# Decay attention and a softplus feed-forward on one core: attention chunks in pairs of two batches

## The chip, the cores and the metric

The kernel runs on one core of a Trainium2 chip. The metric is the device time of one execution in microseconds; three runs of the kernel before gave a median of 625.59 us (625.25 to 626.13). TensorE is called PE below, VectorE DVE, ScalarE ACT, GpSimd POOL, and SP is the engine whose queue issues nearly all DMAs.

## The reference

```python
# q, k, v: (batch 4, heads 8, seq 768, head_dim 64), float32
gamma = 1.0 - 2.0 ** (-5.0 - np.arange(H))          # one decay per head
for t in range(S):
    state = gamma * state + outer(k[t], v[t])        # 64 x 64 per batch and head
    y[t] = q[t] @ state / sqrt(D)
x = y as (3072 tokens, 512)                          # heads side by side
h = x @ w_in                                         # 512 -> 2048
g = np.maximum(h, 0.0) + np.log1p(np.exp(-np.abs(h)))   # softplus
out = g @ w_out                                      # 2048 -> 512
```

The two weight matrices arrive as 64-bit floats, everything else as 32-bit floats.

## The kernel before, in words

**Feed-forward.** The 3072 tokens are worked off in six blocks of 512. A block has 16 steps, one for each 128 of the 2048 hidden features. A step's *hidden group* is 12 matmuls of 128x512 (four slices of x, three products of high and low parts each) into one of two PSUM banks, hp0 and hp1. Then L660 (DVE) and L661 (ACT) make the softplus' correction in the buffer sp, of which there is one; L662 (DVE) reads hp a last time and finishes softplus in sp; L663 (ACT) rounds it to gh and L664 (POOL) takes the remainder to gl. The step's *acc groups* are eight matmuls of gh and four of gl with w_out, into the four banks acc0 to acc3, one for each 128 tokens. After 16 steps acc goes out through w0 or w1. The matmuls of both kinds stand under L343, the helper `mm`.

**Weights.** In block 0 each weight slice is loaded as 64-bit words and turned into a high and a low part (L367 to L391); this uses a bank of a0, a1 for a short while.

**Attention.** The sequences are cut into chunks of 128 positions, six for each batch, 24 in all, four for one block of tokens. `unit` makes one chunk: q, k and v of all heads are loaded (L418, L421) into the buffers qn, kn, vn (two of each), q and v are scaled by powers of the decay (L430, L434), and then PE visits the chunk:

- *transposes* of q and k (T128, L479: four 128x128 for each; or in merged units 64-row pieces, L459), which ACT copies into kt (L486, L487);
- *scores* (Q64): 64x64 matmuls, four side by side, for the scores and for the k-v products of both half chunks. DVE masks the scores into ah (L505) and adds the products to the running state (L514, L516), one state buffer for each half chunk;
- *y* (Q64): state times q, and scores times v. From the sixth unit on ACT copies one part out (L591), DVE adds the other (L597), ACT rounds to x (L600), POOL takes the remainder (L601). Before that L566 and L567 do it.

A visit needs two PSUM banks, of a0, a1 (in the start-up of other banks too). From the twelfth unit on (`MERGED`) the y of a chunk and the transposes of the next one are one planned operation, and the two banks of each step are taken from a0, a1, hp0, hp1 (`WIDE`). `flush` emits a y that is still pending.

**Order.** Nothing is emitted directly. Every operation is given to `Planner` with an engine, a cost, what it comes after, the buffers it uses and a due time, and the planner simulates the five engines: it always takes the operation that can start first, and among those that can start at that time the one with the earliest due time, then the lower number. The resulting order is the order of each engine's queue, SP's DMAs included. An operation that uses several banks starts when all are given back, and a bank is given back when every operation on it has been planned. `waits` holds an operation back for a rival with an earlier due time that wants the same banks within `RESERVE`, or `HOLD` for a patient one. Due times come from a running `now` that advances by 5.44 us a step; `LEAD`, `STAGE` and `EXTRA` place the three steps of a unit against it, `UNIT` and `STEP0` do so in the start-up, whose sequence is `ORDER`. `SLOW` multiplies the costs of ACT, DVE and POOL in the simulation. Each matmul then waits on the chip only for what it itself reads or writes.

In the due times a step's hidden group and the acc groups of the step before it stand side by side:

```python
o = PE(m_ * matmul_time(width, P), group, xs + list(ws) + lasts[-1:], [hp], when[0] + len(lasts))
...
o = PE(m * matmul_time(DM, P), group, need, [acc, gh, gl], when[1] + seq)
...
ffn_step(None, None, i, f, (now - early * step, now + hidden_time + second_time))
```

Of the kernel before, what the change touches and what calls it, by code (L numbers as in the profile page):

```python
# [30 lines left out]
MERGED = 11  # L31
HOLD = 1000
# [21 lines left out]
ENTER = {"R128": 0, "T128": 0, "Q64": 121, "F128": 0}  # L54
LEAVE = {"R128": 0, "T128": 24, "Q64": 202, "F128": 0}
# [46 lines left out]
class Planner:  # L102
# [13 lines left out]
    def order(self):  # L116
# [30 lines left out]
        while len(out) < len(self.ops):  # L147
            best, fits, wants = None, {}, []
            for e, cands in ready.items():
                fits[e] = []  # L150
                for since, op in cands:
                    b = begin(op, since)
                    if op.patient:
                        wants += [(op.due, max(free[e], since), op, u) for u in op.uses if u.slot is None and u.among[0] in SHARED]
                    if b < 1e12:
                        s = max(free[e], b)
                        fits[e].append((s, b, op))
                        if not op.patient:
                            wants += [(op.due, s, op, u) for u in op.uses if u.slot is None and u.among[0] in SHARED]

            def waits(s, op):
                for u in op.uses:
                    if u.slot is None and u.among[0] in SHARED:
                        rivals = sum(d < op.due and t < s + (HOLD if o.patient else RESERVE) and o is not op and not set(v.among).isdisjoint(u.among) for d, t, o, v in wants)
# [58 lines left out]
UNIT = 3000  # L223
STEP0 = 4500
LEAD = -4000
STAGE = 3400
EXTRA = 0.5
# [4 lines left out]
SLOW = 1.02  # L232
# [4 lines left out]
COMFORT = {'PE': 0, 'ACT': 100, 'DVE': 100, 'POOL': 100, 'SP': 0}  # L237
# [3 lines left out]
def decay_attention_then_softplus_ffn(ctx: ExitStack, tc: tile.TileContext, q, k, v, w_in, w_out, qtab, vtab, gtab, out):  # L241
# [53 lines left out]
    hold_st = holder(pool, [P, ND, D], F32, *slots("st", ST))  # L295
# [100 lines left out]
    xdone, xread, stlast, states, ys, pending = {}, {}, {}, {}, [], []  # L396

    def unit(m, first, G, when):

        n = len(ys) + len(pending)  # L400
# [40 lines left out]
        merged = n >= MERGED  # L441
        wide = lambda merged: WIDE if merged and len(ATT[0]) == 2 else ATT[0]
# [6 lines left out]
        i, off = divmod(m * C, T)  # L449
        xt = X[i % 2]  # L450
# [3 lines left out]
        if merged:  # L454
# [6 lines left out]
            tdeps, tuses = ldk + [dq] + old(KT), [*tp, kn, qn]  # L461
            if pending:
                outputs_, cost_, deps_, uses_, _, finish_ = pending.pop()[1:]

                def outputs_and_turn():
                    outputs_()
                    turn()

                tk = tq = PE(cost_ + 58 * 2 * E, outputs_and_turn, deps_ + tdeps, uses_ + tuses, when[0], "Q64")
                tk.patient = True  # L470
                finish_(tk)
            else:
                tk = tq = PE(58 * 2 * E, turn, tdeps, tuses, when[0], "Q64")
            turned = lambda i: bank(tp[i])[:, :2 * E * D].rearrange("p (s e t) -> p s e t", s=2, e=E)
            into = lambda i: buf(kt)[:, :, :E, part(i)]
        else:
# [4 lines left out]
            tk = PE(109 * E, lambda: transposes(0, kn), ldk + old(KT), [tp[0], kn], when[0], "T128")  # L481
            tq = PE(109 * E, lambda: transposes(1, qn), [dq] + old(KT), [tp[1], qn], when[0], "T128")
# [20 lines left out]
        s = PE(2 * E * 117, scores, ck + old(AH) + [dv, *ldk], [kt, kn, vn] + sc, when[1], "Q64")  # L503
# [5 lines left out]
        rows = lambda held: buf(held).rearrange("p (a g) d -> p a g d", a=2)[:, :, first:first + G]  # L509
# [13 lines left out]
        def record(done):  # L523
            for j in range(es.start, es.stop):
                xdone[m, j] = list(done[j % 2])

        if n < FENCED:
            def outputs():
# [8 lines left out]
                def state(r, i, g, a):  # L537
                    add(r, i, g, a, (buf(st[i])[side[r], 2 * a + first + g], buf(kt)[side[r], 1, a * G + g, part(i)]))
# [22 lines left out]
            def finish(y):  # L561
                ys.append(y)
                xdeps = [o for j in range(es.start, es.stop) for o in xread.get((i - 2, j), [])]
# [5 lines left out]
        else:  # L569
            xs = hold_xs()  # L570

            def outputs():
                for g in range(G):
                    for i in range(2):
                        for a in range(2):
                            for r in range(2):
                                if st[i] is not None:
                                    mm(first_half(yp[r])[side[a], 2 * g + i], buf(st[i])[side[r], 2 * a + first + g], buf(kt)[side[r], 1, a * G + g, part(i)], True, True)
# [8 lines left out]
            def finish(y):  # L587
                ys.append(y)
                xdeps = [o for j in range(es.start, es.stop) for o in xread.get((i - 2, j), [])]
# [14 lines left out]
        deps = ma + su[:1] + [dv] + ck + (stlast[m - 1] if c else [])  # L604
        uses = yp + [vn, ah, kt] + [x for x in st[:2] if x]
        pending.append((m, outputs, cost, deps, uses, when[2], finish))
        if n + 1 < MERGED:
            flush()

    def flush():  # L610
        if pending:
            m, outputs, cost, deps, uses, due, finish = pending.pop()
            finish(PE(cost, outputs, deps, uses, due, "Q64"))
# [4 lines left out]
    def ffn_step(s, h, i, f, when):  # L618
        if pending and pending[0][0] < NT * (i + 1):
            flush()  # L620
# [72 lines left out]
        for t in ts:  # L693
# [8 lines left out]
            r = slice(i * T + t * P, i * T + (t + 1) * P)  # L702
# [130 lines left out]
```

## Time and profile before

| | |
|---|---|
| median of three runs | 625.59 us |
| profiled execution: its own time / span of its instructions | 626.27 us / 624.5 us |
| granted PE clock | 1.000 |
| busy PE / DVE / ACT / POOL | 614.5 / 242.3 / 226.7 / 239.8 us |
| HBM traffic | 35.66 MB read, 6.29 MB written |
| wide matmuls (hidden; acc with gh; acc with gl): mean start to start in a row of 12 | 2.72 us for 12 |

In the lines of the profile an instruction is named by its line in the kernel, its engine, its operation and `output<-inputs`, where the names are those of buffers and banks without their numbers. A row of the timeline is start, time until the last one's end, and a count; rows of PE overlap, since matmuls are pipelined and their ends are modelled, so start-to-start is what counts. The square bracket holds the idle time of the engine before the row and what ended it. In the list of waits a line is who waited for whom, the total, the times and the longest. A queue's own lines (SPq) are DMA issues.

### The profile page before, as it was taken

To read this page: it belongs to the slowest core of one execution; us is meant where nothing else is said; L and a number is where in the kernel's file an instruction comes from. 1 tells how busy PE (TensorE), PEld (TensorE's weight loads), DVE (VectorE), ACT (ScalarE), POOL (GpSimd) and SP (SyncE) were. 2 spreads that over 40 slices of the span, in tenths; PEclk is the share of its full clock that TensorE was granted. 3 is DMA by queue.
4 is the path that set the end of the run, shared out by engine and by line. 5 is a ranking of instruction groups with operands and counts; after the bars stand their busy time and mean duration, and the time that the engine had idled before them with its cause. 6 is when DMAs were issued, how large, how long until landed. Compare 5 with 4: busy or idle time off the path is not lost.

```text
span 624.5 us, 13208 instructions
## 1 busy us (share of the span) xinstructions
PE 614.5 (98%) x5619; PEld 500.4 (80%) x5619; DVE 242.3 (39%) x438; ACT 226.7 (36%) x407; POOL 239.8 (38%) x206
## 2 busy tenths in 40 slices
PE   8799999999999999999999999999999999999997
PEld 5678788878888888888888888888888888888886
DVE  3677878643233233332333323324323232322232
ACT  3757778532323233233232332332323331322221
POOL 3667778642233243242332323423323222222221
PEclk9999999999999999999999999999999999999999
DMA  7998385232012023020221210202400000100001
GB/s 187 250 278 257 103 264 186 52 99 72 14 38 52 1 53 102 18 51 8 45 52 68 52 35 18 51 7 45 120 1 18 2 2 0 68 1 1 0 1 67
DMA packets 90442, 42.80 MB, mean 69 GB/s; under 512 B 77072, under 2 KB 85264, under 8 KB 90384
## 3 DMA queue, kind: packets, MB, share of 16 engines
q1 hardware_dynamic: 89936, 41.95, 24.5%
q8 instruction: 44, 0.72, 0.5%
q14 instruction: 14, 0.11, 0.1%
q10 hardware_dynamic: 448, 0.01, 0.0%
HBM read 35.66 MB, written 6.29 MB: 67 GB/s over the span
## 4 chain that ended last, share of the span: by engine, by line
PE 94%; DMA 2%; SPq 2%; ACT 1%; issue 0%; POOL 0%; DVE 0%; POOLq 0%; DVEq 0%
PE hp L343 44%; PE acc L343 42%; PE a L343 5%; PE hp L459 1%; SPq L421 1%; DMA raw<-in_moe_w_out_dram 1%; PE a L479 1%; DMA vn<-in_v_dram 1%; DMA qn<-in_q_dram 0%; SPq L360 0%; SPq L418 0%; PE hp L743 0%; POOL win L391 0%; PE acc L479 0%; DVE sp L660 0%
## 5 line engine op out<-in xcount | busy, mean ns | idle before, releaser
L343 PE MATMUL hp<-x,win 128*128 128x512 f32 (+1 forms) x1176 | 296.2, 388 | 0.1
L343 PEld LDWEIGHTS hp<-x,win 128*128 128x128 f32 x1176 | 215.6, 188 | 44.4 <-DVE x L567 0.3
L664 POOL TENSOR_TENSOR gl<-sp,gh 128x512 fp32r<-128x512 f32 x90 | 116.3, 1293 | 282.7 <-ACT gh L663 205.3
L343 PE MATMUL acc<-wout,gh 128*128 128x512 f32 x736 | 198.9, 393 | 0.6 <-DVE x L567 0.5
L343 PEld LDWEIGHTS acc<-wout,gh 128*128 128x128 f32 x736 | 136.3, 188 | 29.9 <-DVE x L567 0.6
L661 ACT ACTIVATE sp<-sp 128x512 f32<-128x512 f32 x92 | 58.1, 631 | 247.6 <-DVE sp L660 247.6
L660 DVE TENSOR_SCALAR sp<-hp 128x512 uint32<-128x512 uint32 x92 | 63.6, 691 | 188.5 <-PE hp L343 119.2
L343 PE MATMUL acc<-wout,gl 128*128 128x512 f32 x368 | 102.7, 391 | 0.0
L662 DVE SCALAR_TENSOR_TENSOR sp<-hp,sp 128x512 f32<-128x512 f32 x92 | 63.5, 691 | 52.6 <-ACT sp L661 52.2
L343 PEld LDWEIGHTS acc<-wout,gl 128*128 128x128 f32 x368 | 68.8, 188 | 14.9 <-POOL gl L664 0.4
L663 ACT CAST gh<-sp 128x512 fp32r<-128x512 f32 x90 | 55.8, 620 | 56.6 <-DVE sp L662 56.5
L601 POOL TENSOR_TENSOR x<-xs,x 128x512 fp32r<-128x512 f32 x20 | 25.6, 1280 | 37.6 <-ACT x L600 37.5
L597 DVE TENSOR_TENSOR xs<-a,xs 128x256 f32<-128x256 f32 (+1 forms) x40 | 14.3, 400 | 55.7 <-ACT xs L591 55.7
L434 POOL TENSOR_TENSOR qn<-qn,tabs 128x512 f32<-128x512 f32 (+1 forms) x23 | 23.7, 1031 | 17.0 <-DMA qn<-in_q_dram 17.0
L430 POOL TENSOR_TENSOR vn<-vn,tabs 128x512 f32<-128x512 f32 (+1 forms) x24 | 24.2, 1007 | 6.4 <-DMA vn<-in_v_dram 6.3
L367 ACT ACTIVATE raw<-raw 128x512 f32<-128x512 f32 x32 | 21.7, 678 | 10.9 <-DMA raw<-in_moe_w_out_dram 5.5
L391 POOL TENSOR_TENSOR wout<-w,wout 128x512 fp32r<-128x512 f32 x16 | 20.7, 1293 | 6.4 <-ACT wout L390 6.2
L391 POOL TENSOR_TENSOR win<-w,win 128x512 fp32r<-128x512 f32 x16 | 20.7, 1295 | 3.2 <-ACT win L390 3.1
L382 DVE SCALAR_TENSOR_TENSOR a<-raw,a 128x512 uint32<-128x512 uint32 x28 | 19.0, 691 | 1.2 <-ACT a L371 0.7
L387 DVE SCALAR_TENSOR_TENSOR w<-raw,a 128x512 uint32<-128x512 uint32 x28 | 18.7, 682 | 1.0
L600 ACT CAST x<-xs 128x512 fp32r<-128x512 f32 x20 | 12.4, 619 | 14.5 <-DVE xs L597 14.5
L343 PEld LDWEIGHTS a<-kt,st 64*64 64x64 f32 x616 | 11.2, 134 | 7.7 <-issue 6.7
(117 smaller groups left out, 404.6 us busy)
## 6 DMA issues: line engine op xcount, KB each, us to landing
raw<-in_moe_w_in_dram SPq DMA_DIRECT2D x16, 512.0 KB, 5.9
raw<-in_moe_w_out_dram SPq DMA_DIRECT2D x16, 512.0 KB, 6.1
qn<-in_q_dram SPq DMA_DIRECT2D x44, 128.0 KB, 3.2
kn<-in_k_dram SPq DMA_DIRECT2D x44, 128.0 KB, 2.8
vn<-in_v_dram SPq DMA_DIRECT2D x22, 256.0 KB, 3.3
out_dram<-w SPq DMA_DIRECT2D x22, 256.0 KB, 2.1
out_dram<-win SPq DMA_DIRECT2D x2, 256.0 KB, 2.1
qn<-in_q_dram SPq DMA_DIRECT2D x4, 64.0 KB, 2.4
```

Source lines behind the costliest of these rows:

```text
L343: mm = lambda o, l, r, start, stop: emit(nc.tensor.matmul(o, lhsT=l, rhs=r, start=start, stop=stop))
L367: a = ACT(685, lambda word=word: emit(nc.scalar.activation(word(1).bitcast(F32), word(1).bitcast(F32), AF.Copy, scale=2.0**-112)), [ld], [ ...
L382: lambda word=word, wp=wp: emit(nc.vector.scalar_tensor_tensor(bits(wp), word(1), 0x80000000, bits(wp), op0=ALU.bitwise_and, op1=ALU.bitwi ...
L391: low_ = POOL(1300, lambda nm=nm, w=w: emit(nc.gpsimd.tensor_tensor(hl(nm, f)[:, 1], buf(w), hl(nm, f)[:, 0].bitcast(F32), op=ALU.subtract ...
L430: emit(engine.tensor_tensor(heads(held), heads(held), by, op=ALU.mult))
L434: emit(engine.tensor_tensor(all_, all_, by, op=ALU.mult))
L601: xl = POOL(2.53 * E * C, lambda: emit(nc.gpsimd.tensor_tensor(xo(1), buf(xs)[:, :E], xo(0).bitcast(F32), op=ALU.subtract)), [xh] + xdeps, ...
L660: a = DVE(vector_time(T), lambda: emit(nc.vector.tensor_scalar(U(spv()), U(bank(hp)), 0x80000000, None, op0=ALU.bitwise_or)), [lasts[-1]] ...
L661: b = ACT(640, lambda: emit(nc.scalar.activation(spv(), spv(), AF.Softplus)), [a], [sp])
L662: c = DVE(vector_time(T), lambda: emit(nc.vector.scalar_tensor_tensor(spv(), bank(hp), 0.0, spv(), op0=ALU.max, op1=ALU.add)), [b], [hp, sp])
L663: e = ACT(scalar_time(T, False), lambda: emit(nc.scalar.copy(buf(gh), spv())), [c], [sp, gh])
L664: g = POOL(1300, lambda: emit(nc.gpsimd.tensor_tensor(buf(gl), spv(), buf(gh).bitcast(F32), op=ALU.subtract)), [e], [sp, gh, gl])
```

## The change

- Positions 0 to 23 are run through in another order: `TURN` maps position p to chunk m so that batches 0 and 1 take turns chunk by chunk, then batches 2 and 3. Block i of the feed-forward takes positions 4i to 4i+3, and the output rows follow.
- From position 8 on (`PAIRED`) two positions, the same chunk of two batches, are made together. `unit` has become a generator that yields each PE operation's cost, work, predecessors and buffers; `units` joins those of its members into one operation. A pair has three visits: transposes of both (a new kind, S128), scores of both, y of both. The even position has the banks hp0 and hp1 for all three, the odd one a0 and a1; the even one's matmuls are emitted first. Merging y with the next transposes, `pending` and `flush` are gone; positions 4 to 7 are units by themselves as before.
- The state after the first half of a chunk is written into the chunk's k buffer, which is therefore held until y; state buffers are now one for each chunk.
- In `waits`, a patient operation counts as a rival only once the return of its banks is planned, and the time for which it holds others back is 200 ns plus a tenth of its lateness.
- Constants: `UNIT` 3000 to 3400, `STEP0` 4500 to 5600, `LEAD` -4000 to 0, `STAGE` 3400 to 6000, `EXTRA` 0.5 to 0.25, `SLOW` 1.02 to 1.0, `COMFORT` of ACT, DVE and POOL 100 to 0.

```diff
-MERGED = 11
-HOLD = 1000
+PAIRED = 8
+HOLD = 200
...
-                        rivals = sum(d < op.due and t < s + (HOLD if o.patient else RESERVE) and ...
+                        rivals = sum(d < op.due and t < s + (HOLD + max(0.0, s - d) / 10 if o.patient else RESERVE) and ...
...
+    TURN = [NC * (2 * g + a) + c for g in range(B // 2) for c in range(NC) for a in range(2)]
...
-        if (m, 0) not in states:
-            states[m, 0], states[m, 1] = hold_st(), hold_st() if c < NC - 1 else None
-        st = states[m - 1, 1] if c else None, states[m, 0], states[m, 1]
+        if m not in states:
+            states[m] = hold_st() if c < NC - 1 else None
+        st = states[m - 1] if c else None, kn, states[m]
...
-        tp = [hold_bank(wide(merged)) for _ in range(2)]
-        sc = [hold_bank(wide(merged)) for _ in range(2)]
-        yp = [hold_bank(wide(n + 1 >= MERGED)) for _ in range(2)]
+        wide = [["hp0", "hp1"], ["a0", "a1"]][p % 2] if paired and len(ATT[0]) == 2 else ATT[0]
+        tp, sc, yp = [[hold_bank(wide) for _ in range(2)] for _ in range(3)]
...
+            tk = tq = yield 58 * 2 * E, turn, ldk + [dq] + old(KT), [*tp, kn, qn], when[0], "S128"
...
+        s = yield 2 * E * 117, scores, ck + old(AH) + [dv, *ldk], [kt, kn, vn] + sc, when[1], "Q64"
...
+        y = yield cost, outputs, ma + su[:1] + [dv] + ck + (stlast[m - 1] if c else []), yp + [vn, ah, kt] + [x for x in st[:2] if x], when[2], "Q64"
+        finish(y)
+
+    def units(*members):
+
+        running = [unit(*args, len(members) > 1) for args in members]
+        asked = [next(r) for r in running]
+        while asked:
+            costs, runs, deps, uses, dues, kinds = zip(*asked)
+            op = PE(sum(costs), runs[0] if len(runs) == 1 else lambda runs=runs: [run() for run in runs], [d for ds in deps for d in ds], [x for xs in uses for x in xs], min(dues), kinds[0])
+            op.patient = len(members) > 1
+            asked = []
+            for r in running:
+                try:
+                    asked.append(r.send(op))
+                except StopIteration:
+                    pass
...
-            while m < min(target + EXTRA, NB * NT):
-                unit(m, 0, 2, [now + LEAD, now + LEAD + STAGE, now + LEAD + 2 * STAGE])
-                m += 1
+            while m < min(target + EXTRA, NT * (i + 2)):
+                whens = [now + LEAD, now + LEAD + STAGE, now + LEAD + 2 * STAGE]
+                if m >= PAIRED:
+                    units((m, 0, 2, whens), (m + 1, 0, 2, whens))
+                    m += 2
+                else:
+                    units((m, 0, 2, whens))
+                    m += 1
```

More of the change, by code (lines that the diff above doesn't have):

```diff
@@ L157, in order @@
                         fits[e].append((s, b, op))
-                        if not op.patient:
-                            wants += [(op.due, s, op, u) for u in op.uses if u.slot is None and u.among[0] in SHARED]
+                        wants += [(op.due, s, op, u) for u in op.uses if u.slot is None and u.among[0] in SHARED]
             def waits(s, op):
@@ L163, in waits @@
                     if u.slot is None and u.among[0] in SHARED:
-                        rivals = sum(d < op.due and t < s + (HOLD if o.patient else RESERVE) and o is not op and not set(v.among).isdisjoint(u.among) for d, t, o, v in wants)
+                        rivals = sum(d < op.due and t < s + (HOLD + max(0.0, s - d) / 10 if o.patient else RESERVE) and o is not op and not set(v.among).isdisjoint(u.among) for d, t, o, v in wants)
                         if rivals and rivals >= sum(opens(n, op.engine) <= s for n in u.among):
@@ L236 @@
 RAMP = 8
-COMFORT = {'PE': 0, 'ACT': 100, 'DVE': 100, 'POOL': 100, 'SP': 0}
+COMFORT = {'PE': 0, 'ACT': 0, 'DVE': 0, 'POOL': 0, 'SP': 0}
 @with_exitstack
@@ L393, in convert_weights, with unit @@
             wdone[nm, f] = hi, low_
-    xdone, xread, stlast, states, ys, pending = {}, {}, {}, {}, [], []
-    def unit(m, first, G, when):
-        n = len(ys) + len(pending)
+    xdone, xread, stlast, states, ys, count = {}, {}, {}, {}, [], [0]
+    TURN = [NC * (2 * g + a) + c for g in range(B // 2) for c in range(NC) for a in range(2)]
+    def unit(p, first, G, when, paired):
+        n = count[0]
+        count[0] += 1
+        m = TURN[p]
         b, c = divmod(m, NC)
@@ L448, in unit @@
         side = (lo, up)
-        i, off = divmod(m * C, T)
-        xt = X[i % 2]
+        block, off = divmod(p * C, T)
+        xt = X[block % 2]
         old = lambda by: [ys[n - by]] if n >= by else []
         part = lambda i: slice(i * D, (i + 1) * D)
-        if merged:
+        if paired:
             def turn():
@@ L524, in record @@
             for j in range(es.start, es.stop):
-                xdone[m, j] = list(done[j % 2])
+                xdone[p, j] = list(done[j % 2])
         if n < FENCED:
@@ L537, in state @@
                 def state(r, i, g, a):
[L538 removed]
+                    add(r, i, g, a, (state_of(st[i])[side[r], 2 * a + first + g], buf(kt)[side[r], 1, a * G + g, part(i)]))
                 def inner(r, i, g, a):
@@ L562, in finish @@
                 ys.append(y)
-                xdeps = [o for j in range(es.start, es.stop) for o in xread.get((i - 2, j), [])]
+                xdeps = [o for j in range(es.start, es.stop) for o in xread.get((block - 2, j), [])]
                 xo = lambda t, r: xt[:, t, off // W, es.start + r:es.stop:2, off % W:off % W + C]
@@ L588, in finish @@
                 ys.append(y)
-                xdeps = [o for j in range(es.start, es.stop) for o in xread.get((i - 2, j), [])]
+                xdeps = [o for j in range(es.start, es.stop) for o in xread.get((block - 2, j), [])]
                 xo = lambda t: xt[:, t, off // W, es, off % W:off % W + C]
@@ L766, in decay_attention_then_softplus_ffn @@
             first, G = (0, 2) if len(item) == 2 else (int(item[2]), 1)
-            unit(int(item[1]), first, G, [now, now + 1500, now + 2200])
+            units((int(item[1]), first, G, [now, now + 1500, now + 2200]))
             now += UNIT * G
```

56 lines of the change are left out of this document (15 added, 41 removed).

## The prediction

> **What bounds the kernel now.** I read the page first (busy times, the slices, the chain of work that ended last), then the list of waits, then TensorE's timeline around one attention unit, and last what the other engines do at the same moment.
>
> ```profile
> span 624.5 us, 13208 instructions
> PE 614.5 (98%) x5619; PEld 500.4 (80%) x5619; DVE 242.3 (39%) x438; ACT 226.7 (36%) x407; POOL 239.8 (38%) x206
> PE   8799999999999999999999999999999999999997
> PEclk9999999999999999999999999999999999999999
> PE 94%; DMA 2%; SPq 2%; ACT 1%; issue 0%; POOL 0%; DVE 0%; POOLq 0%; DVEq 0%
> ```
>
> TensorE (PE) is full from the third slice on and is 94% of the chain; no other engine passes 39%. So the time is the sum of what PE issues plus the few moments in which it waits, and the change must be priced as PE time: what a visit to attention costs, how many there are, and whether PE now waits inside one. The next fence, from the chain in order of time and then PE's timeline, shows one whole period.
>
> ```profile
> 177.18 2.72 PE hp L343 x12
> 202.21 2.72 PE hp L343 x12
> 162.84 2.88 PE L343 MATMUL hp<-x,win 128*128 128x512 f32 x12
> 165.56 1.98 PE L343 MATMUL acc<-wout,gh 128*128 128x512 f32 x8
> 167.38 1.07 PE L343 MATMUL acc<-wout,gl 128*128 128x512 f32 x4
> 168.38 0.69 PE L343 MATMUL a<-kt,st 64*64 64x64 f32 x32
> 168.89 0.65 PE L343 MATMUL a<-ah,vn 64*64 64x64 f32 x32
> 169.47 0.46 PE L459 MATMUL hp<-ident,kn 64*128 64x64 f32 x8
> 169.77 0.42 PE L459 MATMUL hp<-ident,qn 64*128 64x64 f32 x8
> 170.11 1.20 PE L343 MATMUL acc<-wout,gh 128*128 128x512 f32 x4
> 171.15 1.53 PE L343 MATMUL hp<-x,win 128*128 128x512 f32 x6
> 172.51 0.61 PE L343 MATMUL acc<-wout,gh 128*128 128x512 f32 x2
> 173.57 0.22 PE L343 MATMUL hp<-vn,kn 64*64 64x64 f32 x2
> 173.98 0.23 PE L343 MATMUL hp<-vn,kn 64*64 64x64 f32 x2
> 174.15 0.96 PE L343 MATMUL hp<-x,win 128*128 128x512 f32 x3
> 174.95 0.62 PE L343 MATMUL acc<-wout,gh 128*128 128x512 f32 x2
> 176.10 1.08 PE L343 MATMUL acc<-wout,gl 128*128 128x512 f32 x4
> ACT kt L486 <- PE hp L459: 11.2, 14, 1.0
> ```
>
> What to see. Twelve wide matmuls take 2.72 us, 0.227 each. From 177.18 to 202.21 are 25.03 us; four steps of 24 wide matmuls are 21.76 of them, so 3.27 us is what one unit costs. *Scores visit*: the two acc matmuls at 172.51 end at 172.96, the next wide one starts at 174.15, which is 1.19, and its group of three takes 0.80 instead of 0.68: 1.31 in all. The scores go in groups of four side by side; seven groups lie between 173.57 and 173.98, 0.0586 each, so 16 groups are 0.94 and 0.37 is the price of going in and out. *Merged visit* (y of one chunk, transposes of the next): 167.38 plus four matmuls is 168.29, the next wide one is at 170.11: 1.82, and four that take 1.04 instead of 0.91: 1.95. It holds 0.94 of y, 0.37 of in and out, and 0.64 for the transposes: eight pairs side by side, four pairs in 0.30 with the slow first one (so about 0.065 a pair, 0.5 together) and 0.14 for one more change of array layout. 1.95 + 1.31 is 3.26, the whole 3.27: PE doesn't wait at all here. The last line says that there are 14 merged visits.
>
> **The change, part by part.** *Visits.* Positions 8 to 23 become eight pairs of three visits, 24. For the same chunks there are now 14 merged visits, 16 for scores, two for y alone (the first chunk's and the last's) and two for transposes alone, 34. The older form of transposes is this:
>
> ```profile
> 144.32 0.60 PE L479 MATMUL a<-ident,kn 128*128 128x128 f32 x4
> 144.75 0.60 PE L479 MATMUL a<-ident,qn 128*128 128x128 f32 x4
> 145.11 1.17 PE L343 MATMUL hp<-x,win 128*128 128x512 f32 x4
> ```
>
> That is 0.79, and 0.10 more in the wide matmuls after it (four take 1.17 here, 1.07 at 167.38): 0.89. Before, in sum: 14 x 1.95 + 16 x 1.31 + 2 x 1.31 + 2 x 0.89 = 52.7 us. After, for a pair: scores 32 groups x 0.0586 + 0.37 = 2.25; y the same, 2.25; transposes 16 pairs x 0.065 + 0.37 = 1.41. The last is an operation that never stands alone in this trace. Its going in and out lies between nothing beyond the work (it can't be under 1.0) and the 0.64 - 0.5 = 0.14 of a layout change added to 0.37, so 1.0 to 1.55; I take Q64's 0.37, because the same wide matmuls stand on both sides. A pair is 5.91, eight are 47.3. Gain on paper: 52.7 - 47.3 = 5.4 us, with ends 4.3 and 8.7.
>
> The Trainium skill, TensorEngine Tiling (Array Packing), Key Properties, says that changing the tiling mode drains the array. The rows agree (0.37 for two changes). By that rule alone one counts changes, ten for two units before and six for a pair; at half of 0.37 each the four saved would be 0.74 a pair, an estimate of 5.9 us for eight pairs beside 5.4 from the rows.
>
> *The wait that comes in.* A paired visit takes all four banks, and the even member, which is emitted first, has hp0 and hp1. So the first matmuls of every visit need the bank of the hidden group just finished, and it is free only when VectorE has read it for the last time (L662). The rows of that moment:
>
> ```profile
> 165.13 1.29 POOL L664 TENSOR_TENSOR gl<-sp,gh 128x512 fp32r<-128x512 f32 x1 [5.39 <-ACT gh L663]
> 166.45 0.69 DVE L660 TENSOR_SCALAR sp<-hp 128x512 uint32<-128x512 uint32 x1 [2.16 <-POOL gl L664]
> 167.84 0.69 DVE L662 SCALAR_TENSOR_TENSOR sp<-hp,sp 128x512 f32<-128x512 f32 x1 [0.70 <-ACT sp L661]
> 27.15 0.41 DVE L514 TENSOR_TENSOR st<-acc,st 128x256 f32<-128x256 f32 x1
> 27.62 0.46 PE L343 MATMUL acc<-kt,st 64*64 64x64 f32 x16 [0.45 <-DVE st L514]
> ```
>
> There is one sp buffer. L660 of this hidden group therefore waits until GpSimd has finished the low part of the group before (166.42), and L662 ends at 168.53. PE's visit starts at 168.38. Today nothing is lost: the first half of the visit is y, in a0 and a1, and the transposes into hp come at 169.47. After the change the visit can't begin before 168.53 + 0.06 (the two last rows: st ends at 27.56, PE resumes at 27.62) = 168.59, which is 0.21 late. I expect that at every visit, because the order around one repeats: the planner lets a visit in only when both hp banks are given back. Right after a visit the groups of acc (ready) and of the next hidden group alternate, as at 170.11 to 177.02, and the hidden group ends about 0.9 before the four gl matmuls do; then comes a whole hidden group at once, whose L660 waits for gl as above, then acc, then the visit. 24 x 0.21 = 5.0 us. Ends: 0 (a visit that falls elsewhere) and, if the hidden group ends with the mix instead of 0.9 before it, 1.1 per visit. I take 0.21, which this very place shows.
>
> *What is queued behind it.* PE's queue is in order, so the 0.21 is lost whole: acc of the step is done, and the next gh isn't ready (L663 runs after L662).
>
> *Evacuation.* Per visit ScalarE has four copies instead of two after transposes, VectorE eight operations instead of four after scores; y has four ScalarE copies and four VectorE adds in a row.
>
> ```profile
> 170.22 0.59 ACT L486 COPY kt<-hp 128x512 f32<-128x512 f32 x1 [0.97 <-PE hp L459]
> 170.70 0.59 ACT L487 COPY kt<-hp 128x512 f32<-128x512 f32 x1
> 174.25 0.42 DVE L505 TENSOR_TENSOR ah<-hp,mask 128x256 uint32<-128x256 uint32 x1 [1.62 <-PE a L343]
> 174.59 0.41 DVE L505 TENSOR_TENSOR ah<-a,mask 128x256 uint32<-128x256 uint32 x1
> 174.92 0.41 DVE L514 TENSOR_TENSOR st<-hp,st 128x256 f32<-128x256 f32 x1
> ```
>
> Copies follow each other at 0.48, VectorE's at 0.34: 2.0 and 2.7 us until all is done, while the next use of these engines by the hidden group comes about 4.5 after the visit. PE has four acc groups of two (1.81 us) that need no hp bank, and the first hp bank is back after one copy (0.6) or three VectorE operations (1.2). Cost nothing; if that cover is gone, the mix is reordered and the next visit pays 0.9 more (a rival below).
>
> *State in k's buffer.* No instruction more. But k of a later chunk is loaded only after y instead of after scores, as v is already; q, k and v of a pair are ten DMA issues on SP. In a pair's period of eight steps (43.5 us) y ends some 22 us before the next transposes, and loads land in 3 us. Free. POOL's scaling of them (1.05 each) moves with them into that gap.
>
> *Order of batches, and the constants.* The first two chunks no longer depend on each other, and due times move. PE fully idles only in the first 30 us, and the list of waits sets the scale (1.3, 1.0, 0.8, 0.8, 0.5, 0.5). I take 0, with 1.5 either way. One edge moves: the transposes, scores and y of chunk 8 no longer stand ahead of block 1.
>
> ```profile
> 129.12 1.28 POOL L601 TENSOR_TENSOR x<-xs,x 128x512 fp32r<-128x512 f32 x1
> 133.26 0.98 PE L343 MATMUL hp<-x,win 128*128 128x512 f32 x3
> ```
>
> The last x of chunk 7 is there at 130.40, block 1 begins at 133.26: 2.9 us to spare. Without chunk 8's visits (0.89 + 2 x 1.31 = 3.5) block 1 would begin at 129.8, but chunk 7's y, which stands behind chunk 8's transposes in a0 and a1, comes about 2.4 earlier too. Free, or about 2 us if it doesn't.
>
> **Sum.** The profiled execution took 626.27, its span 624.5. 626.27 - 5.4 + 5.0 = 625.9. The runs' median, 625.59, is 0.7 under that execution, so a median of 625.2.
>
> **The rivals.**
> 1. *The wait isn't there* (faster). If the planner's new due times and holds put a visit where L662 is already done, 5.4 stays: 620.2. For it: the late L662 comes from the particular order mix, hidden, acc. Against: that order is what every merged visit in this trace stands behind, and nothing in the change alters the rule that makes it.
> 2. *Evacuation sets the pace* (slower). If the first hp bank comes back later than the 1.81 us that acc covers, for example because VectorE does the far-off state updates among the first of its eight, the hidden group ends with the mix, gl is 0.9 later and so is L660 of the next group. It decides from 1.81 us after the visit. On the scores visits alone (eight) that is 7 us: about 632; on half of them 629. Against: three operations end at 1.2. The Trainium skill, TensorEngine Tiling (Array Packing), PSUM Bottleneck, speaks for this one: tiling quickens TensorE and not the emptying of PSUM, which may become the limit. No row here shows that limit yet.
> 3. *Block 1 waits for chunk 7* (slower): 2 us, 627.
>
> **How the numbers follow.** 0.2%, 1.25 us, is about what can be told from no change here, so the edges are 624.3 and 626.8. Main case (wait of about 0.2 at most visits, 623.5 to 627): 0.50, of which 0.13 is under 624.3 and 0.05 over 626.8. Rival 1: 0.29, faster. Rival 2: 0.13 and rival 3: 0.08, slower. Faster 0.42, same 0.32, slower 0.26. The range reaches from rival 1 with a little of the unknown start (619.5) to the half case of rival 2 (629); what is left out is the rest of rivals 1 and 2, under 0.2. The likeliest case's own range is 623.5 to 627.
>
> **What would show it.** In the timeline after: three visits for each pair, lasting about 1.0, 2.0 and 2.0 between their first matmul and the next wide one; before each, PE idle with L662 as releaser, 0.1 to 0.25 by the list, or a first start 0.3 after the last gl matmul's end rather than 0.09. Period of a pair: eight steps, 43.5, plus 5.9, plus 0.6. Wrong if the visits start 0.09 after gl (rival 1), if gl of the mix stands before the hidden groups (rival 2), or if PE waits for x at block 1 (rival 3).

## The result, and the profile after

The kernel with the change is slower: median 629.46 us of six executions (628.86 to 629.95) against 625.86 of six of the kernel before (625.25 to 627.47), a ratio of 1.0051 [1.0036, 1.0066]. The prediction was 625.2, "about the same"; 629.46 lies just outside its range. The profiled execution took 629.95, its span is 628.2, and before it was 626.27 and 624.5. So +3.7 is to be explained.

The page of the kernel after:

```profile
span 628.2 us, 13260 instructions
...
PE 615.7 (98%) x5635; PEld 503.1 (80%) x5635; DVE 240.6 (38%) x438; ACT 226.7 (36%) x407; POOL 239.7 (38%) x206
...
PEclk9999999999999999999999999999999999999999
...
q8 instruction: 44, 0.72, 0.5%
```

PE is still the full engine (98%), its granted clock is 0.999 (1.000 before), and the other engines do what they did before. (The helper `mm` is now L340, the last read of hp by DVE is L653, the first is L651.) The list of waits of PE says what is new in it:

```profile
PE acc L340 <- issue: 2.1, 2, 1.3
...
PE acc L340 <- ACT w L690: 0.7, 1, 0.7
PE acc L340 <- DVE w L692: 0.6, 1, 0.6
...
PE hp L340 <- DVE sp L653: 0.5, 2, 0.3
```

The last line is the wait that was forecast, for L653, named only twice. The rest of it doesn't show in this list: it lies inside the visits, between matmuls whose modelled times overlap, and has to be read from start to start. The other lines are three stretches in which PE stands, after block 1 has begun. (Of the two waits in the first line the longer, 1.3, lies in the start, at 17.3 us; the other, 0.9, is the stretch at 421.50.) PE's timeline, at block 1, at one visit of each kind, and at the three stretches:

```profile
129.18 1.07 PE L340 MATMUL acc<-wout,gl 128*128 128x512 f32 x4
130.09 1.75 PE L340 MATMUL hp<-x,win 128*128 128x512 f32 x7
...
163.52 1.07 PE L340 MATMUL acc<-wout,gl 128*128 128x512 f32 x4
164.51 0.88 PE L340 MATMUL hp<-kt 64*64 64x64 f32 x30
...
166.78 1.45 PE L340 MATMUL acc<-wout,gh 128*128 128x512 f32 x5
...
176.93 1.07 PE L340 MATMUL acc<-wout,gl 128*128 128x512 f32 x4
177.93 0.59 PE L340 MATMUL hp<-kt,st 64*64 64x64 f32 x5
...
180.25 1.43 PE L340 MATMUL acc<-wout,gh 128*128 128x512 f32 x5
...
190.36 1.07 PE L340 MATMUL acc<-wout,gl 128*128 128x512 f32 x4
191.35 0.69 PE L457 MATMUL hp<-ident,kn 64*128 64x64 f32 x8
191.85 0.44 PE L457 MATMUL hp<-ident,qn 64*128 64x64 f32 x8
...
192.73 1.20 PE L340 MATMUL acc<-wout,gh 128*128 128x512 f32 x4
...
340.00 0.84 PE L340 MATMUL hp<-x,win 128*128 128x512 f32 x3
341.52 0.73 PE L340 MATMUL acc<-wout,gh 128*128 128x512 f32 x2 [0.68 <-ACT w L690]
...
420.93 0.96 PE L340 MATMUL acc<-wout,gh 128*128 128x512 f32 x3
422.77 0.96 PE L340 MATMUL acc<-wout,gh 128*128 128x512 f32 x3 [0.88 <-issue]
...
544.15 0.39 PE L340 MATMUL acc<-wout,gl 128*128 128x512 f32 x1
545.12 0.73 PE L340 MATMUL acc<-wout,gh 128*128 128x512 f32 x2 [0.58 <-DVE w L692]
```

DVE's timeline at the last of these visits, the transposes:

```profile
189.38 0.69 DVE L651 TENSOR_SCALAR sp<-hp 128x512 uint32<-128x512 uint32 x1 [2.12 <-POOL gl L655]
190.77 0.69 DVE L653 SCALAR_TENSOR_TENSOR sp<-hp,sp 128x512 f32<-128x512 f32 x1 [0.70 <-ACT sp L652]
```

*The start.* Block 1 begins at 130.09, before at 133.26: 3.17 gained, close to the 129.8 that the prediction gave for it.

*The visits.* Four gl matmuls from 190.36 would end at 191.27, and the visit's first matmul starts at 191.35. DVE's last read of hp ends at 191.46, because its first read had waited for GpSimd, as forecast. The first eight transposes take 0.50 from start to start; by the single records the first of these steps is 0.256, so PE goes on at 191.61, 0.146 after the read has ended. Read the length of a visit as the distance between the wide matmuls on its two sides, less 0.91 for the four gl matmuls: transposes 1.47 to 1.52 where they wait (1.24 in the two of eight visits where the bank is free), scores 2.36, y 2.42, and 2.71 and 2.70 for two visits of y in the middle of a block. (Two visits for scores and one of y have 96 matmuls instead of 128 and are shorter, 2.25 and 1.95.) In all but the two free visits of transposes there is one long step near the beginning, and in each of these 22 PE goes on 0.146 after DVE's last read has ended.

*The stretches.* From start to start they are 1.07 (340.46 to 341.52), 1.27 (421.50 to 422.77) and 0.97 (544.15 to 545.12), where a usual step of wide matmuls is 0.23. The second step after each stop is 0.11 longer than usual. Together the three cost 2.9 beyond the usual steps.

*Where it went, by the blocks.* Block 1 begins 3.17 earlier; from the start of block 1 (130.09; 133.26) to that of block 5 (533.50; 530.84) it is 403.41 against 397.58, 5.83 more; from there to the end 1.01 more, most of it the third stretch. -3.17 + 5.83 + 1.01 = 3.67.

### The profile page after: what moved, and what is told of

It is laid out like the page before. It is cut to its first block, busy times and chain, and to the rows that moved or that the text cites. A ratio compares the mean times of both kernels' runs of the same rounds, so it can differ in the third digit from the quotient of the medians.

```text
span 628.2 us, 13260 instructions
## 1 busy us (share of the span) xinstructions
PE 615.7 (98%) x5635; PEld 503.1 (80%) x5635; DVE 240.6 (38%) x438; ACT 226.7 (36%) x407; POOL 239.7 (38%) x206
## 5 line engine op out<-in xcount | busy, mean ns | idle before, releaser
L340 PE MATMUL hp<-x,win 128*128 128x512 f32 (+1 forms) x1176 | 290.4, 386 | 1.0 <-POOL win L388 0.5
L340 PEld LDWEIGHTS hp<-x,win 128*128 128x128 f32 x1176 | 216.8, 188 | 45.5 <-POOL win L388 0.9
L340 PE MATMUL acc<-wout,gh 128*128 128x512 f32 x736 | 197.6, 395 | 2.1 <-issue 0.9
L340 PEld LDWEIGHTS acc<-wout,gh 128*128 128x128 f32 x736 | 135.4, 188 | 32.8 <-issue 1.3
L651 DVE TENSOR_SCALAR sp<-hp 128x512 uint32<-128x512 uint32 x92 | 63.5, 691 | 247.4 <-PE hp L340 167.1
L340 PE MATMUL acc<-wout,gl 128*128 128x512 f32 x368 | 102.6, 390 | 0.0
L653 DVE SCALAR_TENSOR_TENSOR sp<-hp,sp 128x512 f32<-128x512 f32 x92 | 63.5, 691 | 52.6 <-ACT sp L652 52.4
L340 PEld LDWEIGHTS acc<-wout,gl 128*128 128x128 f32 x368 | 69.0, 188 | 14.4
L491 DVE TENSOR_TENSOR ah<-a,mask 128x256 uint32<-128x256 uint32 x28 | 10.6, 416 | 6.9 <-PE a L340 6.9
L583 DVE TENSOR_TENSOR xs<-a,xs 128x256 f32<-128x256 f32 (+1 forms) x24 | 8.8, 408 | 9.8 <-ACT xs L577 9.8
## 6 DMA issues: line engine op xcount, KB each, us to landing
vn<-in_v_dram SPq DMA_DIRECT2D x22, 256.0 KB, 4.2
out_dram<-w SPq DMA_DIRECT2D x22, 256.0 KB, 2.2
out_dram<-win SPq DMA_DIRECT2D x2, 256.0 KB, 2.1
```

Of the source, the lines that this page charges most:

```text
L340: mm = lambda o, l, r, start, stop: emit(nc.tensor.matmul(o, lhsT=l, rhs=r, start=start, stop=stop))
L651: a = DVE(vector_time(T), lambda: emit(nc.vector.tensor_scalar(U(spv()), U(bank(hp)), 0x80000000, None, op0=ALU.bitwise_or)), [lasts[-1]] ...
L653: c = DVE(vector_time(T), lambda: emit(nc.vector.scalar_tensor_tensor(spv(), bank(hp), 0.0, spv(), op0=ALU.max, op1=ALU.add)), [b], [hp, sp])
```

## Experiments

The expectations name the theories by letters. A: the visits wait for hp at their head, so what hides or removes that wait gives about 5 back. The rivals put the loss elsewhere; the one that lasted longest is C, that the new order and constants cost it. Each run below has its own runs of the kernel before beside it, and ratios are against those.

**1. The odd member first.** The odd member's banks a0, a1 are free long before; its matmuls now go ahead of those that need hp.

```diff
-lambda runs=runs: [run() for run in runs]
+lambda runs=runs: [run() for run in reversed(runs)]
```

> The changed kernel, with the matmuls of the odd position (banks a0, a1) emitted ahead of the even one's (hp0, hp1) in each paired visit; the planned order of everything else stays. Theory A (PE waits 0.2 to 0.3 us in 22 of 24 visits, because the first matmuls need the hp bank that VectorE still reads; measured 6.4 us in sum from the visits' lengths): the wait is covered by the odd member's 0.5 to 1.0 us, so 629.5 - 6.4 = about 623. Theory B (what is lost is idle time at block edges and in the start, through the new order): the visits' waits are hidden anyway or come back elsewhere, 629 to 630.

622.13 us (621.86 to 622.69), 0.993 [0.9917, 0.9944] of before. That is 7.3 less than the kernel after. Its timeline of PE at the same three visits:

```profile
162.69 1.07 PE L340 MATMUL acc<-wout,gl 128*128 128x512 f32 x4
163.69 0.69 PE L340 MATMUL a<-kt 64*64 64x64 f32 x32
...
165.73 1.45 PE L340 MATMUL acc<-wout,gh 128*128 128x512 f32 x5
...
175.88 1.07 PE L340 MATMUL acc<-wout,gl 128*128 128x512 f32 x4
...
178.92 1.43 PE L340 MATMUL acc<-wout,gh 128*128 128x512 f32 x5
...
189.03 1.07 PE L340 MATMUL acc<-wout,gl 128*128 128x512 f32 x4
190.03 0.46 PE L457 MATMUL a<-ident,kn 64*128 64x64 f32 x8
...
191.18 1.20 PE L340 MATMUL acc<-wout,gh 128*128 128x512 f32 x4
```

DVE's last read at the first of them:

```profile
163.11 0.69 DVE L653 SCALAR_TENSOR_TENSOR sp<-hp,sp 128x512 f32<-128x512 f32 x1 [0.70 <-ACT sp L652]
```

From the gl matmuls to the next wide ones: scores 163.52 to 166.78 = 3.26 after, 162.69 to 165.73 = 3.04 here; y 3.32 and 3.04; transposes 2.37 and 2.15. Nothing else of the three visits differs, DVE's last read still ends about 0.2 after the gl matmuls would (163.80 against 163.60 at the first), and it is now covered by the odd member's work. Over all 24 visits the lengths fall from 49.6 to 43.6, by 6.0. So theory A holds, and the wait costs 6.0, not 5.0. The other 1.3 of the 7.3 is mostly the stretch at 421.50, which is gone too (it wasn't aimed at); the one at the edge of blocks 2 and 3 is 0.82 here, that of 4 and 5 0.93.

**2. The same wait put into the kernel before.** There the merged visit does y first and the transposes into hp second; this turns them round.

```diff
+                    turn()
                     outputs_()
-                    turn()
```

> The kernel before, with the two halves of each merged visit exchanged: transposes into hp0, hp1 first, y in a0, a1 second. Nothing else changes. Theory A: in the 11 or so merged visits that stand 0.16 us ahead of VectorE's last read of hp, PE now waits 0.25 each as in the changed kernel: + 2.8, about 628.5. Theory B: no change, 625.9 within 0.6.

632.05 (631.25 to 632.73), 1.0088 [1.0072, 1.0103]: +5.5, twice the expected. PE's timeline at an ordinary merged visit and at one right after a block's edge:

```profile
167.38 1.07 PE L343 MATMUL acc<-wout,gl 128*128 128x512 f32 x4
168.37 0.73 PE L459 MATMUL hp<-ident,kn 64*128 64x64 f32 x8
...
170.38 1.19 PE L343 MATMUL acc<-wout,gh 128*128 128x512 f32 x4
...
244.33 0.27 PE L459 MATMUL hp<-ident,kn 64*128 64x64 f32 x1
245.37 0.43 PE L459 MATMUL hp<-ident,kn 64*128 64x64 f32 x7 [0.77 <-DVE sp L662]
```

The gl matmuls and the next wide one are 3.00 apart here, 2.73 in the kernel before (167.38 to 170.11): 0.27 more, where 0.21 is what L662 is late by. Eleven such visits are 3.0. Three more, each the first merged visit after a block's edge, stand 1.04 at their first step: there the visit follows the hidden group more closely, and L662 ends at 245.22, 0.89 after the visit has begun. They make 2.9. So the price of the wait is confirmed in a kernel that has nothing else of the change, and it isn't its lateness alone: here too PE goes on 0.15 after the read has ended (245.22 to 245.37).

**3. The old constants in the kernel after.**

```diff
-UNIT = 3400; STEP0 = 5600; LEAD = 0; STAGE = 6000; EXTRA = 0.25; SLOW = 1.0; COMFORT = 0
+UNIT = 3000; STEP0 = 4500; LEAD = -4000; STAGE = 3400; EXTRA = 0.5; SLOW = 1.02; COMFORT = 100 (ACT, DVE, POOL)
```

> The changed kernel with the constants of before (UNIT, STEP0, LEAD, STAGE, EXTRA, SLOW, COMFORT). Theory A: the visits' waits stay, so at best the idle stretches (2.9 us) go: 626.5 to 629.5. Theory B (the constants' order is what costs): 625 or less, that is, most of the 3.6 us goes.

630.77 (628.12 to 634.13), 1.0068 [1.0043, 1.0093], above what either theory expected. Scores and y wait as before (2.36 to 2.41 and 2.42), so that wait isn't made by the constants. The start is much worse: block 1 begins at 136.43 instead of 130.09, with 2.93 of it for the first pair's transposes, which stand ahead of block 1 here; idle stretches of 1.5 and 2.1 lie at 30.7 and 36.4. After it, this kernel is quicker: 493.0 to the end instead of 498.1, 1.5 of it the visit moved out, and it has none of the three idle stretches, and transposes that mostly wait less. So the new constants are worth several microseconds at the start, and the idle stretches come with them. What in the constants makes them is not shown: in this run no output transfer takes over 2.81, so it doesn't tell whether the old constants would leave room for a longer one.

**4. The state in k's buffer alone, in the kernel before.**

```diff
-            states[m, 0], states[m, 1] = hold_st(), hold_st() if c < NC - 1 else None
-        st = states[m - 1, 1] if c else None, states[m, 0], states[m, 1]
+            states[m] = hold_st() if c < NC - 1 else None
+        st = states[m - 1] if c else None, kn, states[m]
```

> The kernel before, with the state of the first half chunk in k's buffer alone: no pairs, batches in the old order. Theory A: k is loaded after y instead of after scores, with over 10 us to spare; 625.9 within 0.8. Rival (the longer hold of k delays the start or block 0): 627 or more.

627.62 (625.73 to 630.08), 1.0018 [1.0005, 1.0031]. That is 1.1 more than before (0.3 to 1.9 by the interval), and not free. Block 1 begins at 133.80 instead of 133.26, and from there to the end both take 491.3. So what can be placed of it, 0.5, lies in the start, and it is small.

**5. Two buffers sp in the kernel after.** L651 then no longer waits for GpSimd. A buffer xs is given up for the room.

```diff
-XS = 2
+XS = 1
-    hold_sp = holder(pool, [P, T], F32, "sp0")
+    hold_sp = holder(pool, [P, T], F32, "sp0", "sp1")
```

> The changed kernel with two sp buffers instead of one (a second xs buffer is given up for the room). Then L651 (L660 of before) need not wait for GpSimd's gl, VectorE's last read of hp ends 2.35 us after the hidden group, and the acc groups of a step last 2.72. Theory A (the wait at the head of the visits is VectorE's late read, late because sp is single): the visits lose their 0.27 each, 6.0 in sum, less up to 1 for the missing xs buffer: 623 to 625. Rival (the visits wait for the bank itself or for the change of array layout, not for VectorE): 629 to 631.

624.57 (622.75 to 627.58), 0.9973 [0.9953, 0.9992]. DVE's timeline, then PE's, at one visit of transposes:

```profile
350.53 0.69 DVE L651 TENSOR_SCALAR sp<-hp 128x512 uint32<-128x512 uint32 x1 [1.55 <-PE hp L340]
351.92 0.69 DVE L653 SCALAR_TENSOR_TENSOR sp<-hp,sp 128x512 f32<-128x512 f32 x1 [0.70 <-ACT sp L652]
```

```profile
352.85 0.46 PE L457 MATMUL hp<-ident,kn 64*128 64x64 f32 x8
353.14 0.42 PE L457 MATMUL hp<-ident,qn 64*128 64x64 f32 x8
```

L651 now follows the hidden matmuls, L653 ends at 352.61, before the visit begins at 352.85, and the first eight transposes take 0.29 instead of 0.50, with hp still first. Scores and y take 2.12 each, transposes 1.24 (three of them 1.74, with a stop of 0.53). From block 1 to block 5 it is 397.44, 6.0 less than after. Of these 6.0 the visits give 4.8 (their lengths fall from 49.6 to 44.8; at the three of 1.74 the read is still late), and the rest lies in the stretches: those at the edges are gone, and one of 1.04 stands at 306.74. Part is given back in the start (block 1 at 132.40). This is the second way of taking the wait off, by its cause and not by its cover, and it works wherever the read comes in time.

**6. Odd member first, and more buffers for the output.** The copies of acc may go to xs0 and xs1 in all blocks, beside w0 and w1. It asks whether the edges are the rest of the loss.

```diff
             if i == NB - 1:
                 ob.among += ["win1", "win2"]
+            else:
+                ob.among += ["xs0", "xs1"]
```

> The odd-first version, in which the output copies of blocks 0 to 4 may also use xs0 and xs1, so that the third and fourth copy need not wait for the first two outputs' transfers. Theory: the idle PE at 337.0 and 536.2 us (0.6 and 0.7 beyond the usual spacing) comes from that wait, in one case behind a transfer of instructions; 622.1 - 1.3 = 620.8. Rival (the idle moves to another place, for example copies that come in the way of softplus): 622 or more.

619.92 (619.76 to 621.82), 0.9904 [0.9881, 0.9927]: 6.1 below the kernel before, the best of all. After 31 us no step between two matmuls is longer than 0.35. Block 1 begins at 128.78, 4.48 earlier than before; from there to block 5 it is 395.57, 2.01 less than before; the rest is equal. With the waits and the stretches gone, the span is 6.5 under that of before (618.0 against 624.5): 5.5 of it by the 24 visits against the old ones, and 1.0 in the start. So the gain on paper, 5.4, is there.

**7. The output buffers alone.** The edit of 6 without that of 1.

> The changed kernel with the same wider choice of output buffers and the even position first as it was. Theory A: the visits' waits stay, only the edges' idle (0.84 and 0.74) goes: 629.5 - 1.5 = 628.0. Rival (the edges carry the loss): under 626.5.

627.49 (626.95 to 628.1), 1.0017 [1.0004, 1.003], 2.0 less than after. The stretches at the edges are gone, though the first edge's transfers took 4.56 to 4.99 and the last one's 3.9 to 4.33: with more buffers PE doesn't wait for them. Two stretches without a releaser (0.96 at 361.25, 0.79 at 476.85) are there in place of the one at 421.50. The first:

```profile
362.22 0.96 PE L340 MATMUL acc<-wout,gh 128*128 128x512 f32 x3 [0.57 <-issue]
```

-7.3 for run 1 and -2.0 here are -9.3; together, in run 6, it is -9.5.

**8. The order of batches alone, in the kernel before.**

```diff
+    TURN = [NC * (2 * g + a) + c for g in range(B // 2) for c in range(NC) for a in range(2)]
...
+        m = TURN[p]
```

> The kernel before, with the batches in turn (the new order of chunks) alone, without pairs. Expected from the prediction's zero for this part: 626.3 within 1.0. Rival (the new order of chunks and its loads cost the idle in the start and at the edges): 628 or more.

629.45 (628.26 to 631.03), 1.0051 [1.0034, 1.0068]: the rival's size, not the zero of the prediction. PE's timeline in the start:

```profile
34.81 0.98 PE L343 MATMUL acc<-ah,vn 64*64 64x64 f32 x32
38.27 0.63 PE L482 MATMUL a<-ident,kn 128*128 128x128 f32 x4 [2.47 <-issue]
```

Block 1 begins at 138.03 instead of 133.26, and from there to the end the span is that of the kernel before (491.3 in both). The order with the old constants costs its 4.8 in the start alone (2.9 by the medians).

**9. The output buffers in the kernel before.**

> The kernel before, with xs0 and xs1 as further output buffers of blocks 0 to 4. If the loss at the block edges belongs to the changed kernel's order alone, nothing to gain: 626.0 within 0.7. Rival (the edges cost the kernel before as much): 624.5 or less.

627.04 (625.77 to 627.61), 1.0012 [1.0002, 1.0021]: nothing gained. The edges are no cost of the kernel before.

**10. Order and constants without the pairs.** The edit of 8, and all seven constants as after.

> The kernel before, with the batches in turn and all constants of the changed kernel, but without pairs. The batches in turn alone cost 3.4, nearly all before block 1 (which began at 138.0 instead of 133.3). Theory C (the constants make up for that, so order and constants together are about nothing in the start): block 1 begins at 133 to 134.5, 626 to 627.5. Rival (they don't): 628.5 to 631.

639.43 (638.98 to 641.96), 1.0219 [1.0196, 1.0242], far above what either side expected. The start is repaired, block 1 at 132.27 instead of 138.03, as expected of C; the total isn't. The list of waits of PE begins

```profile
PE hp L343 <- DVE sp L665: 3.8, 11, 0.3
PE acc L343 <- POOL gl L667: 2.0, 3, 0.7
```

With these constants the planner puts the old visits where hp or gl is still being made, and a merged visit takes 2.20 instead of 1.83, one for scores 1.59 instead of 1.18 (lengths between the wide matmuls, as above). At three places PE stands for gl, steps of about 1.1 from start to start. Constants and visits are a set; the parts can't be added.

**11. The kernel after again, unaltered**, to see whether the three idle stretches are accidents of one execution.

> The changed kernel once more, unaltered, beside the others of this call: 629.5 within 0.7. If the idle PE at the two block edges (from 340.5 and 544.2) is the program's, it is there again within 0.2; the idle without a releaser at 421.5 should be there again too if it is the program's, and elsewhere or nowhere if it is chance.

629.36 (628.54 to 630.61), 1.005 [1.0035, 1.0065]. All three are there: 340.51 to 341.53, 421.47 to 422.60, 543.94 to 544.65.

**12. The same with 64 more instructions on PE early on.** The stretch at 340.46 can be followed back. The third output copy waits for w, that is for a transfer. ACT's timeline, SP's, and the DMA rows of 336.5 to 341.5 in the kernel after:

```profile
336.12 0.59 ACT L690 COPY w<-acc 128x512 f32<-128x512 f32 x1 [0.67 <-PE acc L340]
...
340.88 0.58 ACT L690 COPY w<-acc 128x512 f32<-128x512 f32 x1 [3.65 <-DMA out_dram<-w]
```

```profile
336.73 5.09 SPq L694 DMA_DIRECT2D out_dram<-w  x3
```

```profile
q8 instruction: 1, 0.02, 1.8%
...
out_dram<-w SPq DMA_DIRECT2D x3, 256.0 KB, 4.0
```

The transfer lands after 4.0 instead of 2.2 (the page's median for it, `out_dram<-w SPq DMA_DIRECT2D x22, 256.0 KB, 2.2`). One packet of the instruction queue q8, 16 KB, lies in that stretch; it begins at 337.82 and takes 1.46 us. The transfer issued at 336.73 is completed in sixteen parts: by the trace's records of completion fifteen are there within 2.10 us, the last only after 4.05. So one part of sixteen is held up while a packet is under way. The trace doesn't name the DMA engine of either. Another such packet lies at 420.0 to 421.2, just ahead of the stretch that has no releaser. If the packets are the cause, shifting the stream of instructions against the work moves the stretches. Sixteen of the filler's matmuls get two tiny ones more each, 64 instructions with their weight loads.

```diff
-lambda n=n: emit(nc.tensor.matmul(bank(idles)[:, :n], ...
+lambda n=n, i=i: [emit(nc.tensor.matmul(bank(idles)[:, :w_], ...)) for w_ in ([n, 16, 16] if 8 <= i < 24 else [n])]
```

> The changed kernel with 32 tiny matmuls (16 columns) more among the idle-time matmuls of the first 20 us; the planned order is the same, but all of PE's later instructions lie 64 instructions further on. If PE stands still at 421.5 for 1.0 us because its next 16 KB of instructions aren't there yet (they are fetched at 419.9 to 421.1, right after a visit of 256 instructions), that idle goes or stands behind another visit, and the output transfer that a fetch held up at 337.8 is free or another is held up. Rival (a wait inside the plan): idle again at 421.5 within 0.5. Total 628 to 630.5, up to 1.5 of it from the start.

628.40 (626.43 to 631.42), 1.0048 [1.0027, 1.0069]. In the profiled execution, which took 626.43, all three stretches are gone. Its ACT and PE at the same edge:

```profile
338.48 0.59 ACT L690 COPY w<-acc 128x512 f32<-128x512 f32 x1 [1.73 <-DMA out_dram<-w]
```

```profile
339.53 0.84 PE L340 MATMUL hp<-x,win 128*128 128x512 f32 x3
340.21 0.61 PE L340 MATMUL acc<-wout,gh 128*128 128x512 f32 x2
```

The transfer lands in time, all sixteen parts by 2.12, and the instruction packets near these places lie at 332.58, 353.24, 419.69, 437.19 and 533.35. The waits in the visits are what they were (1.51, 2.36, 2.41). The profiled execution's span is 624.7, 3.5 under that of the kernel after, and the stretches were 2.9. The median falls by only 1.1, and the executions spread from 626.43 to 631.42, so what the shift is worth on the whole is not settled by this run.

That a packet goes with the late part of a transfer is seen again at the other edge of the kernel after (540.20) and at the first one in runs 1, 7 and 11: fifteen parts come within 2.09 to 2.27, the last after 3.80 to 4.56, each time with a packet under way. That PE stands at 421.50 for want of instructions is named by no row, but the traces say more than one packet near by. Count PE's instructions in order of time, 11 270 matmuls and weight loads and its queue's own 152 waits, 11 422 in all; the page has 44 packets of 16 KB. The last one before the stretch at 421.50 is number 8641, which is 33 x 256 + 193, and exactly 33 packets have ended by then. In run 11 it is number 8641 again, in run 7 they are 7361 and 9665, in run 5 it is 6337: each 193 beyond a multiple of 256 (28, 37 and 24 times 256), and 28, 37 and 24 packets have ended. Each time PE goes on 1.4 to 1.6 after the end of the last of these packets, and each time a visit of 256 matmuls and weight loads has just gone by. So PE stands each time at the same place in a run of 256 instructions, and goes on soon after the packet of the same number has come. That PE waits for instructions there is as good as shown.

## Why the prediction was wrong, point by point

*Gain on paper, 5.4: right.* Run 6 has the 24 visits without their waits. Counted with the slower wide matmuls behind them, the old visits of these chunks take 51.9 in the kernel before and the new ones 46.4 in run 6: 5.5. (Its median is 6.1 under before; the rest lies in the start.) The visit that never stood alone, transposes of a pair, takes 1.24 plus 0.11 in the wide matmuls behind it, 1.35 against 1.41; scores and y take 2.13 and 2.14 plus the same 0.11, 2.25 against 2.25.

*The rule on the drain.* The Trainium skill, TensorEngine Tiling (Array Packing), Key Properties, says that a change of tiling mode drains the array; counted by changes alone the gain came out at 5.9, from rows at 5.4. The visits' 5.5 lies nearer to the rows, but 0.4 is too little here to tell them apart firmly.

*The wait that comes in, 24 x 0.21 = 5.0: right in place and cause, too small by 0.9.* In 20 visits the first matmul starts 0.11 to 0.16 before DVE's last read ends, for the reason given (L651 behind GpSimd through the one sp); in two of y it is 0.45, and two of transposes are free. Run 1 covers the wait and takes 6.0 off the visits, and run 5 removes its cause and takes off 4.8, for three visits stay late. The step that was too small is the handover, the time from DVE's end to PE's next matmul. The prediction took 0.06 from one row (27.56 to 27.62); in all 22 visits it is 0.146, which leaves 0.12 beyond the lateness. So an ordinary visit loses 0.23 to 0.28, each of the two late ones 0.56, and the sum is 5.9.

The traces show what the row at 27.62 lacks. In each of the 22 visits PE's queue carries an instruction of its own for the wait, 0.051 long, ahead of the weight load; at the transposes:

```profile
L457 PEldq EVENT_SEMAPHORE  x16: 51/51/51, 150.1 to 489.1; - x16
```

In the kernels before and after and in runs 2, 3, 5, 7 and 10, take every idle time of PE over 0.1 that DVE ends. The 40 with such an instruction end 0.145 to 0.147 after DVE does, the 18 without it 0.053 to 0.058. The 40 hold hidden groups of run 10 too, in which nothing of the group had begun, so the price is that of the wait and not of a burst that is broken off.

*Order of batches, and the constants, "0, with 1.5 either way": the step that failed outright.* The prediction priced them as one small unknown of the start, and took its scale from the list of waits of the kernel before. The start came nearly as forecast (130.09 against 129.8), but by two terms that nobody had forecast and that cancel, which is luck: the order alone costs 4.8 there in a profiled execution (run 8), and the constants win it back (runs 3 and 10). What they do to the later blocks was not looked at. The runs show 2.9 in three stretches after block 1. At two block edges the output copies, which have two buffers w, wait for a transfer that takes 4.0 instead of 2.2 because one part of it is held up beside an instruction packet. The third stands where PE's count of instructions is 193 beyond a multiple of 256 (run 12). The edges were to be had only if one asked who else uses ACT and DVE near hp: the prediction treated the evacuation of attention and never the evacuation of acc. Run 7 takes the two edges away with more buffers, and in run 12 they are gone with the packets elsewhere, so this is one loss seen from two sides: too little slack for a transfer of 2.2 us, and something that makes it 4.0. Where the packets would fall could not be read off any line of the prediction, and the execution of run 12 without the stretches, 626.43, lies inside its likeliest range. So the mechanism of the stretches was missed, and that they all came is in part bad luck.

*Evacuation at nothing: right.* The Trainium skill, TensorEngine Tiling (Array Packing), PSUM Bottleneck, spoke for the rival that copying out of PSUM would set the pace; no visit of any of these kernels shows it.

*State in k's buffer at nothing: not quite.* In the kernel before it costs 1.1 (run 4), of which 0.5 is seen in the start.

*The rivals.* The first, no wait, didn't come by itself; two visits of transposes only. It came when made (run 1). The second and the third didn't occur.

*The sum as it came.* In the profiled executions: the visits -5.5, their waits +5.9, the three stretches +2.9, and 0.3 in the start, where chunk 8's visits took 3.5 and block 1 begins only 3.17 earlier. That is +3.6 against +3.7 measured and -0.4 forecast. The misses are the stretches (2.9 for a term that stood at 0), the waits (0.9) and the start (0.3).

## What to carry to other kernels

When several members share one visit to an engine, the visit inherits the latest reader of any of its buffers; emit first the member whose buffers were free first. Here the order of two closures is worth 7 us, 6 of them in the visits, and turns a loss of 0.5% into a gain of 0.7%. A planner that sees the joint visit as one operation can't see this: read the beginning of the visit from matmul to matmul, since overlapping records hide a stop of 0.25 us from the list of waits. Price a stop at its lateness plus the handover (0.12 here), and when due times move, follow every user of the engines in question through the block's edge, the output's too.

## What was not expected of the hardware

- A wait for which PE's queue carries an instruction of its own ends 0.145 to 0.147 after the engine waited for, one without such an instruction 0.053 to 0.058 (58 waits for DVE in seven traces). A bank that is 0.11 to 0.16 late costs a visit 0.23 to 0.28.
- One 16 KB packet of the instruction queue (1.46 us) went with a 256 KB output transfer that took 4.0 us instead of 2.2, in the same place in two executions of the same kernel. Fifteen of the transfer's sixteen parts came in time, and one was late.
- PE can stand about 1 us with no releaser in the profile (421.50 to 422.77, shortly after a visit of 256 matmul and weight-load instructions); it is gone when the stream is shifted by 64 instructions. All five such stretches, in four executions, stand 193 instructions beyond a multiple of 256, and PE goes on 1.4 to 1.6 us after the end of the instruction packet of that number (the 33rd at 33 x 256 + 193). That it waits for instructions wasn't tried directly.
